# Expert 1's first eight slices in one visit of each token block instead of two, in a newly written order

## The chip, the cores and the metric

The kernel runs on one core of a Trainium2 chip. Its engines are named as the profile names them: PE (TensorE, matrix products), DVE (VectorE), ACT (ScalarE), POOL (GpSimd) and SP (SyncE, which issues all the transfers here). The time is the device time of one execution in microseconds (us); the median of several runs counts. Beside it stands the profile of one execution.

## What is computed

Causal attention with a bias from a running sum, then two feed-forward experts one after the other, on 2304 tokens of width 512:

```python
# q, k, v: [4, 8, 576, 64]; s: [4, 8, 576]
s_pos = np.maximum(s, 0.0)
cum = np.cumsum(s_pos, axis=-1)
bias = -(cum[:, :, :, None] - cum[:, :, None, :])
scores = np.where(causal, -1000000000.0, scores + np.minimum(bias, 0.0))
...
x = attention output as [2304, 512]
# expert 1: w_in [512, 2048], w_out [2048, 512]
h = x @ w_in
x = (h - np.tanh(h)) @ w_out
# expert 2: w_in [512, 1024], w_out [1024, 512]
h = x @ w_in
solu = h * softmax(h)
out = (layer_norm(solu) * g_ln) @ w_out
```

All products keep nearly full 32-bit precision: an operand is split into a high and a low part, and each product is three matmuls (high by high, high by low, low by high).

## The kernel before

**Attention.** There are 16 pairs of heads (four pairs for each of four batch items). They make 20 jobs: the first item's four pairs are done in two jobs each (jobs 0 to 3 take its first 256 tokens, 4 to 7 the rest), the other twelve pairs in one each (8 to 19). A job goes through its query rows 64 at a time: scores on PE (L715, masked by L723), the bias and the row minimum on DVE (L732), the exponential with its sum on ACT (L743), the reciprocal on DVE (L656, L659), the scaling on POOL (L747), transposes on PE (L781), copied out by ACT (tile pt, L294), and then weighed by v on PE (L821). The result goes out to memory (tensor xd).

**Expert 1.** The tokens are cut into nine blocks of 256, the inner width of 2048 into sixteen slices of 128. A block and a slice together are 24 matmuls: 12 for h (L868, "h part") and 12 that add into the output in the accumulator acc (L891, "x2 part"), with tanh on ACT (L873), the difference on DVE (L877), the high part by ACT (L294, tile gh) and the low part by DVE or POOL (L313, L314) between the two. The weights come as 64-bit numbers and are converted slice by slice, by ACT, DVE and now and then POOL (tiles cd, ct; wih, wil, woh, wol), early in the kernel for slices 0 to 7, later for 8 to 15.

While attention still runs there is room in memory for the weights of slices 0 to 7 alone. They are gone through in visits: `VISITS = ((0, 4), (4, 8))` means that every block is visited twice, once for slices 0 to 3 and once for 4 to 7. A visit loads the block of x from xd (tile xb, L860; block 0's first visit finds it in place), and at its end `keep_part` reads acc: the first visit copies it to the tile xp (`keep`, on ACT) and stores it to the tensor pd (L959); the second loads it back (L940), adds acc to it on DVE (L953) and stores it again. There is a single acc, so a visit's first x2 part waits until the one before it has been read out. After attention the slices 8 to 15 follow in a visit of their own (accumulator big), which loads the kept sum for the last time and goes straight on to expert 2 (L1016 and L1134 on PE).

**The order.** Nothing at run time decides the order. `schedule` makes all the steps with what they depend on, and the table `ORDER` of some 3300 numbers, written into the kernel, says in which order their instructions are issued, so what each engine does one after the other. A `+20` in it means 20 matmuls on a tile of zeros (L558), which keep PE busy where it is expected to wait. The costs in the code (`t_score`, `t_pe` and the like) belong to the planning of such a table; the order issued is that of the table alone.

Of the kernel before, what the change touches and what calls it, by code (L numbers as in the profile page):

```python
# [9 lines left out]
F32R = mybir.dt.float32r  # L10
# [30 lines left out]
VISITS = ((0, 4), (4, 8))  # L41
FA = 8
LT = ("cd", "cu")
TB = 256
# [5 lines left out]
0 f 3 u i l x 49 4i 7x p r +20 13 10 1u 2i 16 86 1a 1c 1x 39 bu 2l 4d 6 2p 1f 20 3c 4l 2r 23 1i 4f 1l 89 3f 2u 26 2x  # L50
29 bx 3i 81 +7 1o 3l 83 30 1r ff +1 2c 9 3o 2f +1 33 bl 36 +1 3r 3u +1 4r 31x 5i jc 4u 8f 3x 4y 50 5l 32l 8i 8m 5o 53
c 56 96 5r 8o 59 5u 66 8r 40 99 5x 9u 4o 43 9c al 8u 69 46 8x bp 6x 9x 6f a1 br c3 8c a3 5c 70 90 cu 5f a6 c6 c0 73 ca
di 6d a9 6i cx 60 ac 320 6l fc 76 ao e9 d0 6o 79 dl 63 7c af d3 cc 9f d6 9i 6r cf ar ec d9 7f ci f9 6u au 9l ax ef 323
+2 9o cl ei 7i el 93 b0 +2 7l 9r fi 32o 326 eo ai b3 7o 329 j9 co b6 er n9 7r dc cr b9 eu 32c r6 df dr 7u 32r fl bc du
32u 32f bf gc 32x hi 32i dx 330 bi e0 gf 333 fo 339 gi fs 336 jf fu hr fx j6 +7 ji +1 k9 hl g0 ho gl g3 v3 hu gr 11o
gp dp +4 g6 n6 gu hx e3 gx h0 i0 e6 i3 g9 +4 ex h9 if r3 33c h3 hc i6 h6 +1 ii 33f hf v0 33i i9 f0 35x il f3 33l +1 io
ic 3cl ir 33o 33r f6 ki iu 3co km 33u ko n3 jl 3cr jr 33x kc lf 3cu ju jp jx kf 3cx 50l k0 nf kr ix ku lo l6 k3 j0 189
3du li k6 kx lr ll j3 l0 lu 3d0 lx l3 m0 m3 11l o6 360 363 3d3 186 l9 mc 3d6 3d9 m6 366 lc mf 3dc m9 369 ml mi 36c mo
pc 36f nc ni o9 no mr 36i r0 oc pl 340 nr nm nu of nx 359 pf ol rc po 1er pi s3 oj oo 343 or mu 346 o0 pr p3 mx 1eu
349 o3 p6 ou pu px n0 p9 34c ox q0 34f ux v9 34i p0 q3 q9 3ec q6 11i sc sg si s6 rf 399 s9 t9 rj sl rl so ro sr 35c rr  # L60
11u 1lf qi tc ru ql qc ti 1lc tf t0 rx tl t3 qf 35f 35i su to qo 35l sx tr t6 35o s0 tu 34l 35r tx r9 vc w0 qr u6 12l
w3 vi w9 w6 u0 qu 35v wf vl u9 vo wi u3 vg uf vr wl qx 11x uc 121 wo 12u 13r ui 12o wx 130 v6 wd vu 12y 123 140 x0 vx
wr 12r 144 159 126 13u x3 129 133 13x 136 12c 16f wu 15i 13i 146 139 15m 15o 11r 149 12f 15c 13c 14c 13l 16o 12i 14o
13f 16i 13o x6 15f 14f 16r 14r 1s0 34o 15r xf 14i yo 15u 16u xj 34r 15x x9 183 xl 18f 34u ul 166 16l yr yx 1rx 14l xc
34x 1eo yu xo 350 14u 160 uo xr 18c 16x 169 z1 170 xu 353 ur 14x 356 163 uu 16c 173 196 150 xx 153 39c 3df y3 y0 39f
z3 17c z6 36l 18i 1f0 39i 3di yc z9 156 18m 18o 19f zc 199 19l 17l 18r 3dl 3dx zl 18u 19c 19j 17o 18x 19o yf 19r 39l
3do y6 3e0 19u yi 190 176 3dr 193 1ex 17f 1a3 y9 3e3 179 1f3 3ef 39o 17i 1l9 1f7 1f9 1fc 3e6 1ac 1ff 39r 3e9 379 1fi
1bu 3er 39u 36o 3h0 1al 17r 1ap 1ar 1af yl 1bx 1ai 1c3 1c0 1c7 1au 36r 1c9 1ax 19x 1li 36u zf 1b9 1cc 17u zo 1cf 1a0
17x zi 1fl 1b0 1a6 1bc 1fo 36x 1a9 1b3 1bf 1ll 180 1cr 1fr 1b6 1lo 1gx zr 370 1lu 1if 1ci 1g0 3b9 373 1h0 1lx 1bi 376
1g6 1h3 1m0 1io 1cl 1m3 37c 3ei 1ls 1is 1bl 37f 1iu 1bo 1h6 1br 1co 1ha 1m6 37i 1hc 1cu 1fu 1mc 37l 1m9 1cx 3eu 1hf  # L70
37o 1fx 3el 1hi 1ml 37x 1hu 1mf 1ii 37r 3f9 1hl 1g9 1mr 1gc 1mp 37u 1il 1gf 1ho 1ix 1mi 3fo 1g4 1go 1j0 1mu 3ex 3eo
# [167 lines left out]
def t_turn(n, k=1):  # L239
    return t_pe(109.0 * k, 128 * k)  # L240
# [1077 lines left out]
```

## Time and profile before

| | |
|---|---|
| median of 3 runs | 781.69 us (779.96 to 782.26) |
| the profiled execution, its own time | 778.94 us |
| its span, first to last instruction | 777.2 us |
| PE busy | 764.8 us of the span (98%) |
| PE weight loads busy | 676.8 us (87%) |
| DVE / ACT / POOL busy | 565.0 / 409.8 / 119.5 us |
| moved by DMA | 111.90 MB |
| granted PE clock | 1.00 throughout |

The busy time of an engine is the union of its instructions' records. The span lies within the profiled execution's own time; 1.74 us are around it. The profiled execution was somewhat faster than the median of the three timed ones, by 0.35%.

### The profile page before, as it was taken

What the parts mean: (1) busy time and instruction counts of PE and PEld (TensorE: products, weight loads), DVE (VectorE), ACT (ScalarE), POOL (GpSimd) and SP (SyncE); (2) the same over time, 40 slices, a digit from 0 to 9 for tenths busy, and PEclk for the clock granted to TensorE, in tenths of its full rate; (3) what the DMA queues carried; (4) which work ended last, traced back from release to release, by engine and by line L of the source; (5) the groups of instructions that cost most, each with busy time, mean ns of one, the idle gap of its engine ahead of it and who ended that gap; (6) DMA issues with size and microseconds to landing.
All of it is one profiled execution on the core that took longest, in us unless ns stands there. A gap on an engine that the chain in (4) does not pass through costs nothing.

```text
span 777.2 us, 16641 instructions
## 1 busy us (share of the span) xinstructions
PE 764.8 (98%) x6239; PEld 676.8 (87%) x6239; DVE 565.0 (73%) x1647; ACT 409.8 (53%) x1030; POOL 119.5 (15%) x193
## 2 busy tenths in 40 slices
PE   8899999999999999999999999999999999999997
PEld 5566788879889899999999898898888899989986
DVE  6888989654564458786699998869496755586783
ACT  6789989775665545454465663423243332343431
POOL 3235354431230200000000000001020001010000
PEclk9999999999999999999999999999999999999999
DMA  7999979874444278876535522112000310110001
GB/s 202 293 302 257 316 235 314 258 209 158 154 140 155 85 252 266 262 261 215 180 123 181 167 83 55 35 48 82 28 28 28 96 55 14 42 55 28 20 36 41
DMA packets 90033, 111.90 MB, mean 144 GB/s; under 512 B 11792, under 2 KB 74256, under 8 KB 89952
## 3 DMA queue, kind: packets, MB, share of 16 engines
q1 hardware_dynamic: 89952, 110.83, 46.2%
q8 instruction: 49, 0.80, 0.4%
q14 instruction: 32, 0.26, 0.1%
HBM read 87.11 MB, written 23.70 MB: 143 GB/s over the span
## 4 chain that ended last, share of the span: by engine, by line
PE 88%; DVE 5%; ACT 2%; DMA 2%; issue 1%; SPq 1%; POOL 0%; DVEq 0%; ACTq 0%; POOLq 0%
PE t L868 23%; PE big L891 13%; PE t L1134 12%; PE acc L891 11%; PE t L821 6%; PE big L1016 6%; PE t L781 5%; PE t L715 5%; PE b L1016 4%; PE t L1120 2%; ACT U L743 1%; DMA bc<-cum_d 1%; DMA cum_d<-pt 1%; ACT pt L294 1%; DVE U L732 1%
## 5 line engine op out<-in xcount | busy, mean ns | idle before, releaser
L868 PE MATMUL t<-xb,wih 128*128 128x256 f32 x1152 | 202.5, 279 | 0.0
L868 PEld LDWEIGHTS t<-xb,wih 128*128 128x128 f32 x1152 | 175.0, 188 | 1.7 <-DVE r L656 0.2
L868 PE MATMUL t<-xb,wil 128*128 128x256 f32 x576 | 159.5, 277 | 0.0
L868 PEld LDWEIGHTS t<-xb,wil 128*128 128x128 f32 x576 | 108.3, 188 | 0.0
L747 POOL TENSOR_SCALAR U<-U,r 128x64 f32<-128x64 f32 (+8 forms) x144 | 82.8, 589 | 163.5 <-DVE r L659 50.2
L891 PE MATMUL acc<-gh,woh 128*128 128x256 f32 x576 | 102.6, 280 | 0.8 <-DVE xp L953 0.7
L891 PE MATMUL big<-gh,woh 128*128 128x256 f32 x576 | 101.0, 278 | 0.0
L873 ACT ACTIVATE th<-t 128x256 f32<-128x256 f32 x144 | 54.7, 381 | 77.1 <-PE t L868 69.7
L877 DVE TENSOR_TENSOR g<-t,th 128x256 f32<-128x256 f32 x144 | 59.5, 417 | 46.6 <-ACT th L873 45.3
L294 ACT CAST gh<-g 128x256 fp32r<-128x256 f32 x144 | 58.1, 406 | 65.1 <-DVE g L877 32.4
L743 ACT ACTIVATE U<-U,m 128x64 f32<-128x64 f32 (+8 forms) x144 | 80.1, 558 | 21.2 <-DVE m L732 20.7
L891 PEld LDWEIGHTS big<-gh,woh 128*128 128x128 f32 x576 | 87.8, 188 | 1.0
L891 PEld LDWEIGHTS acc<-gh,woh 128*128 128x128 f32 x576 | 87.0, 188 | 1.7 <-ACT th L873 0.8
L891 PE MATMUL acc<-gh,wol 128*128 128x256 f32 x288 | 79.8, 277 | 0.4 <-DVE wol L313 0.4
L891 PE MATMUL big<-gh,wol 128*128 128x256 f32 x288 | 79.9, 277 | 0.0
L313 DVE TENSOR_TENSOR gh<-g,gh 128x256 fp32r<-128x256 f32 x124 | 54.0, 439 | 28.2 <-ACT gh L294 27.1
L732 DVE CUSTOM_DVE_ANT_0 U<-bc,t 128x64 f32<-128x64 f32 (+8 forms) x144 | 60.2, 441 | 8.3 <-PE t L723 6.6
L314 POOL TENSOR_TENSOR gh<-g,gh 128x256 fp32r<-128x256 f32 x20 | 16.5, 827 | 316.9 <-ACT gh L294 249.6
L294 ACT COPY pt<-t 128x512 f32<-128x512 f32 (+4 forms) x160 | 60.0, 428 | 7.2 <-PE t L781 6.4
L715 PE MATMUL t<-kn,q 64*64 64x288 f32 (+8 forms) x640 | 58.9, 422 | 2.3 <-DVE wol L313 1.3
L891 PEld LDWEIGHTS acc<-gh,wol 128*128 128x128 f32 x288 | 54.1, 188 | 0.6 <-DVE wol L313 0.6
L891 PEld LDWEIGHTS big<-gh,wol 128*128 128x128 f32 x288 | 54.2, 188 | 0.0
(114 smaller groups left out, 1433.8 us busy)
## 6 DMA issues: line engine op xcount, KB each, us to landing
xb<-xd SPq DMA_DIRECT2D x17, 1024.0 KB, 6.1
cd<-in_moe_w_in_dram SPq DMA_DIRECT2D x24, 512.0 KB, 4.8
cd<-in_moe_w_out_dram SPq DMA_DIRECT2D x24, 512.0 KB, 5.0
bc<-cum_d SPq DMA_DIRECT2D x32, 288.0 KB, 6.4
pd<-xp SPq DMA_DIRECT2D x18, 512.0 KB, 3.8
xp<-pd SPq DMA_DIRECT2D x18, 512.0 KB, 3.6
xd<-xs SPq DMA_DIRECT2D x16, 320.0 KB, 4.5
kn<-in_k_dram SPq DMA_DIRECT2D x16, 288.0 KB, 6.6
```

The source lines that it names most:

```text
L294: then(nc.scalar.copy(o, i) if scale == 1.0 else nc.scalar.activation(out=o, in_=i, func=AF.Copy, scale=scale))
L313: return self.any([("dve", t_dve(n, pair=True), lambda: nc.vector.tensor_tensor(*views(), op), "diff-dve"), ("pool", t_pool(n) + split, la ...
L715: nc.tensor.matmul(X[a][c, :z - a], lhsT=V["q"][r, o:o + 64], rhs=V["k"][r, a:z], start=True, stop=True, skip_group_check=True)
L732: nc.vector.tensor_tensor_reduce(out=X["u"][:, a:z], in0=V["bc"][:, n, a:z], in1=X[b][:, a - b:z - b], scale=-0.125, scalar=X["m"] if "m" ...
L743: nc.scalar.activation(out=X["u"][:, :nk], in_=X["u"][:, :nk], func=AF.Exp, scale=-1.0, bias=X["m"], accum_out=Y["s"][:, n:n + 1])
L747: eng.tensor_scalar(X["u"][:, :nk], X["u"][:, :nk], Y["r"][:, n:n + 1], 1.0, ALU.mult, ALU.mult)
L868: nc.tensor.matmul(ps, lhsT=w[l][:, k, f * 128:f * 128 + 128], rhs=xb[:, r, k, :], start=k == 0 and x == 0, stop=k == 3 and x == 2)
L873: nc.scalar.activation(out=X["th", f], in_=X["h", f], func=AF.Tanh)
L877: nc.vector.tensor_tensor(X["g", f], X["h", f], X["th", f], ALU.subtract)
L891: nc.tensor.matmul(X["acc"][:, m, :], lhsT=w[l][:, f, m * 128:m * 128 + 128], rhs=X["gh", f][:, r, :], start=f == c0 and m % 2 == 0 and x ...
L1016: i = nc.tensor.matmul(o, lhsT=self.x2[j][:, l, x, k], rhs=r[:, b, k, :], start=start and k == 0 and n == 0, stop=k == 1 and n == 2, skip_ ...
L1134: nc.tensor.matmul(X["po"], lhsT=X["lt", k // 4][:, l, k % 4, :], rhs=r[:, k, :], start=k == 0 and a == 0, stop=k == 7 and a == 2)
```

## The change

`VISITS` has one entry in place of two: each block goes through slices 0 to 7 in one visit. So there are nine visits and not eighteen before slices 8 to 15: nine loads of x fewer, and no kept sum is loaded back and added in this part, nor stored a second time; what is stored is the copy of acc after eight slices. Which of two pools a block of x lies in is counted from the other end. The costs used in planning are other numbers (they issue nothing), and the table ORDER is a new one, with 47 matmuls on zeros where there were 53. The products, the conversions of weights, attention and expert 2 have the same steps as before, in another order.

```diff
-VISITS = ((0, 4), (4, 8))
+VISITS = ((0, 8),)
...
-0 f 3 u i l x 49 4i 7x p r +20 13 10 1u 2i 16 86 1a 1c 1x 39 bu 2l 4d 6 2p 1f 20 3c 4l 2r 23 1i 4f 1l 89 3f 2u 26 2x
...
 def t_score(n, rows):
-    t = 1.6667 * n + 119.0 if rows == 1 else {192: 393.0, 320: 599.0, 448: 868.0, 576: 1090.0}[n]
+    t = 1.6667 * n + (160.0 if n < 128 else 180.0 if n < 256 else 150.0) if rows == 1 else {192: 535.0, 320: 685.0, 448: 912.0, 576: 1150.0}[n]
...
     def x_tile(self):
         n, self.nx = self.nx, self.nx + 1
-        return self.sb(self.xo if n % 2 and n < len(VISITS) * self.NB else self.mo, [128, 2, 4, TB], "xb", F32R, 1)
+        return self.sb(self.xo if n % 2 == 0 and n < len(VISITS) * self.NB else self.mo, [128, 2, 4, TB], "xb", F32R, 1)
...
-                s = add("pe", t_pe(1370.0, 12 * TB), lambda f=f: h_part(f), ld + [w["ready"][2 * f]] + list(deps), acq=("ps",),
+                s = add("pe", t_pe(1372.0, 12 * TB), lambda f=f: h_part(f), ld + [w["ready"][2 * f]] + list(deps), acq=("ps",),
```

The order shows what moves in three places. Line numbers are two smaller in the changed kernel. First the transfers that SP issues in the middle of attention, before: xd is where attention's results lie, xb a block of x, pd the kept sums.

```order
L834 DMA xd_73<-xs 256x1x256
L959 DMA pd_77<-xp 128x1024
L940 DMA xp<-pd_75 128x1024
L860 DMA xb<-xd_72 128x8x256
L588 DMA v<-in_v_dram 128x4x128
L590 DMA v<-in_v_dram 64x128
L834 DMA xd_73<-xs 256x1x320
L860 DMA xb<-xd_72 128x8x256
L834 DMA xd_74<-xs 256x1x256
L602 DMA bc<-cum_d 64x1152 x2
L959 DMA pd_75<-xp 128x1024
```

And about the same place, where the third block's sum is stored, now:

```order
L832 DMA xd_73<-xs 256x1x320
L832 DMA xd_73<-xs 256x1x256
L957 DMA pd_77<-xp 128x1024
L586 DMA v<-in_v_dram 128x4x128
L588 DMA v<-in_v_dram 64x128
L832 DMA xd_73<-xs 256x1x320
L832 DMA xd_74<-xs 256x1x256
L832 DMA xd_73<-xs 256x1x256
L600 DMA bc<-cum_d 64x1152 x2
```

The load of the kept sum, the second load of the same block and the second store of pd_75 are gone; the rest of the queue has closed up.

Second, ACT some way ahead of the weighing of job 10's second part. Before, the first accumulator had been copied out here and the second block had begun (th and gh are expert 1's, U and pt attention's, wih and ct the weights'):

```order
L743 ACTIVATE U,s<-U,m 128x128
L294 COPY xp<-acc 128x1024
L294 CAST wih_95<-ct 128x4x128
L743 ACTIVATE U,s<-U,m 128x192
L743 ACTIVATE U,s<-U,m 128x384
L743 ACTIVATE U,s<-U,m 128x128
L873 ACTIVATE th<-t 128x256
L294 COPY pt_1767<-t 128x4x64
L873 ACTIVATE th<-t 128x256
L294 CAST gh<-g 128x256
L873 ACTIVATE th<-t 128x256
L294 CAST gh<-g 128x256 x2
```

ACT now, at the same weight's conversion:

```order
L741 ACTIVATE U,s<-U,m 128x384
L741 ACTIVATE U,s<-U,m 128x448
L292 CAST wih_95<-ct 128x4x128
L292 COPY pt_1836<-t 128x4x64
L741 ACTIVATE U,s<-U,m 128x512
L415 ACTIVATE ct<-cd 128x512
L292 CAST xs<-t 128x256
L741 ACTIVATE U,s<-U,m 128x320
L292 COPY pt_1855<-t 128x2x64
L741 ACTIVATE U,s<-U,m 128x576
L741 ACTIVATE U,s<-U,m 128x256
L871 ACTIVATE th<-t 128x256
```

Attention has moved ahead of expert 1 here. Counted over the whole order up to that weighing on PE, expert 1 has had 9 h parts and 8 x2 parts before, 5 and 4 now; ACT has 198 steps ahead of it and not 207 (four tanh, five casts of gh, one copy of acc and one cast of a weight fewer, one exponential and one cast of xs more).

Third, DVE after attention, before: here the second visits' sums are added between the conversions of weights.

```order
L877 TENSOR_TENSOR g<-t,th 128x256
L399 TENSOR_SCALAR ct<-ct 128x512
L953 TENSOR_TENSOR xp<-acc,xp 128x1024
L402 TENSOR_SCALAR ct<-ct 128x512
L399 TENSOR_SCALAR ct<-ct 128x512
L405 SCALAR_TENSOR_TENSOR ct<-cd,ct 128x512
```

Now the accumulator is read by ACT, and DVE has no such row before slices 8 to 15. ACT there:

```order
L871 ACTIVATE th<-t 128x256
L292 CAST gh<-g 128x256
L292 COPY xp<-acc 128x1024
L871 ACTIVATE th<-t 128x256
L292 CAST woh_4949<-ct 128x512
```

The reading of acc has moved from DVE's queue, behind a conversion step, to ACT's, behind a cast of gh.

## Rows read from the trace of the kernel before

**Rows 1.** The page, part 1: busy us (share of the span) xinstructions.

```profile
PE 764.8 (98%) x6239; PEld 676.8 (87%) x6239; DVE 565.0 (73%) x1647; ACT 409.8 (53%) x1030; POOL 119.5 (15%) x193
```

**Rows 2.** Busy time by stretch: PE, PEld, DVE, ACT, POOL, PEclk, DMA share, GB/s.

```profile
34.50:113.80 79.30, 77.61 (x800) 59.24 (x800) 69.23 (x271) 69.25 (x203) 34.55 (x54) 1.00 0.96 280
0.00:60.00 60.00, 54.06 (x505) 36.84 (x506) 46.54 (x193) 44.24 (x131) 21.97 (x48) 1.00 0.94 265
60.00:140.00 80.00, 79.41 (x858) 61.98 (x857) 70.61 (x280) 71.99 (x217) 37.34 (x57) 1.00 0.96 282
140.00:280.00 140.00, 139.55 (x1393) 121.88 (x1392) 72.26 (x285) 85.82 (x256) 32.55 (x59) 1.00 0.52 158
280.00:360.00 80.00, 79.20 (x695) 78.67 (x694) 64.52 (x135) 41.30 (x92) 2.03 (x2) 1.00 0.83 271
360.00:480.00 120.00, 119.58 (x976) 116.06 (x975) 105.78 (x232) 65.22 (x139) 5.37 (x6) 1.00 0.45 143
480.00:777.20 297.20, 292.98 (x1824) 261.36 (x1823) 205.28 (x528) 101.21 (x198) 20.26 (x21) 1.00 0.13 42
```

**Rows 3.** The same view, the densest stretch for ACT.

```profile
60.00:100.00 40.00, 39.48 (x429) 29.17 (x428) 35.37 (x161) 38.23 (x124) 18.37 (x33) 1.00 1.02 295
```

**Rows 4.** PE's waits: engine, line, waited for: us in total, times, longest.

```profile
PE t L781 <- POOL U L747: 1.8, 5, 0.5
PE t L715 <- DVE wol L313: 1.3, 1, 1.3
...
PE acc L891 <- DVE xp L953: 0.7, 1, 0.7
PE t L715 <- DMA kn<-in_k_dram: 0.5, 1, 0.5
```

**Rows 5.** PE in order of time: start, us, form, count [idle before].

```profile
297.11 0.28 PE L891 MATMUL acc<-gh,wol 128*128 128x256 f32 x1
...
300.85 0.28 PE L891 MATMUL acc<-gh,wol 128*128 128x256 f32 x1
```

**Rows 6.** All instructions on the tile xp: ns least/median/most, first to last start.

```profile
L959 SPq DMA_DIRECT2D pd<-xp x18: 319/331/1453, 97.5 to 374.5; - x18
L940 SPq DMA_DIRECT2D xp<-pd x18: 320/327/486, 124.8 to 700.7; - x18
L294 ACT COPY xp<-acc x9: 987/1012/1020, 96.5 to 364.5; 128x1024 f32<-128x1024 f32 x9
L953 DVE TENSOR_TENSOR xp<-acc,xp x9: 1212/1218/1225, 143.2 to 373.2; 128x1024 f32<-128x1024 f32 x9
```

**Rows 7.** PE at the one long wait for the accumulator.

```profile
336.21 0.28 PE L868 MATMUL t<-xb,wil 128*128 128x256 f32 x1
337.15 0.47 PE L891 MATMUL acc<-gh,woh 128*128 128x256 f32 x2 [0.66 <-DVE xp L953]
```

**Rows 8.** DVE at that wait.

```profile
334.95 0.92 DVE L399 TENSOR_SCALAR ct<-ct 128x512 f32<-128x512 f32 x1
335.79 1.21 DVE L953 TENSOR_TENSOR xp<-acc,xp 128x1024 f32<-128x1024 f32 x1
```

**Rows 9.** PE at the start.

```profile
1.10 4.45 PE L558 MATMUL acc<-junk 128*128 128x256 bf16 x20 [1.10 <-POOL junk L553]
5.48 0.48 PE L715 MATMUL t<-kn,q 64*64 64x64 f32 x4
...
7.44 0.94 PE L558 MATMUL acc<-junk 128*128 128x256 bf16 x7
8.90 0.33 PE L781 MATMUL t<-idn,U 128*128 128x128 f32 x1 [0.52 <-POOL U L747]
```

**Rows 10.** Tiles th and gh from 34.5 us to the weighing at 113.8.

```profile
L873 ACT ACTIVATE th<-t x9: 371/383/400, 36.2 to 107.7; 128x256 f32<-128x256 f32 x9
L294 ACT CAST gh<-g x9: 387/407/424, 38.0 to 110.0; 128x256 fp32r<-128x256 f32 x9
```

**Rows 11.** PE where job 10's second part is weighed.

```profile
113.78 2.79 PE L821 MATMUL t<-pt,v 128*64 128x320 f32 x22
```

More of the change, by code (lines that the diff above doesn't have):

```diff
@@ L55 @@
[L55 to L59, printed above, removed]
@@ new lines @@
+1li 1gc 1bc 37f 1fo 1m6 373 1go 1hf 1cl 1hi 1cu 37i 1m9 3b9 1bf 1hu 1gr 1cx 1if 376 1gu 1gf 1co 1mc 37l 17u 1gi 1hl
+17x 3fc 1gl 1ml 180 1mf 1mr 1ii 1mi 1d0 1io 1il 37o 1iu 1mu 1ho 1mp 37x 1mx 1d3 37r 1n0 1ni 1yl 1n9 1hr 1ix 1d9 1d6
+1yi 1i3 37u 3bc 1nr 1nc 1i6 1j0 1n3 1nv 3ef 1dc 1nx 1jc 1nl 1ru 1n6 1j3 1df 1i9 3bf 1jl 1no 1di 1is 3bi 1ic 3ei 1dl
+3bl 380 256 1nf 1dx 1ju 1jo 253 1do 1e0 1jx 1jr 383 1yf 1dr 3el 1e3 1e6 386 1yr 1e9 3bo 1s6 1du 389 3br 39x 1ec 1o0
+38c 3eo 1k0 1o3 3bu 38l 38f 1of 1k3 1s9 1k6 1sf 1sd 1hx 1s3 1k9 1ef 1si 1sl 1j6 1i0 1ei 1ki 1jf 1j9 1el 1kc 3er 1ji
@@ new lines @@
+3h9 3ar 3gx 3cf 3h0 3au 3h3 3ho 3ci 3hc 213 3ax 216 3i6 3h6 3hr 3b0 3hf 3b3 3hu 3io 219 3i9 200 3b6 21l 203 10c 10f
+3j6 20f 3ir 21c 206 10i 3gf 10r 209 10l 3hi 20i 20c 3hl 10o 21o 3ic 3gi 21r 3j9 20l 3jo 3hx 3gl 3i0 3iu 3k6 3go 3jr
+3l3 3i3 3li 3if 3ii 3jc 3lx 3k9 3il 3j3 3ix 3j0 3ju 3jl 3l6 3jf 3ji 3kc 3k3 3jx 3ll 3k0 3l9 3kl 3m0 3kf 3ki 3lo 3ko
+3lc 3lf 3m3 3kr 3lr 3lu 10u 3m6 110 21f 3ku 3m9 3mf 3kx 21i 113 10x 3mc 3mi 3ml 116 3mo 3mr 226 2bu 119 11c 23c 229
+11f 22f 22c 1sx 2ox 22j 23l 21u 22l 23f 2ou 3mu 21x 22o 23o 23i 22r 1t6 2i6 22u 220 1tc 1t0 233 3nc 1t3 223 1ta 23r
@@ L161 @@
+796 7ec 79a 786 7ei 789 7el 79c 7eo 7eu 78c 79f 7er 79i 7ff 7ex 78f 7f0 7f3 78i 7f6 79u 7fo 7f9 79l 7fc 79x 79o 79r
+7fi 7a0 7fr 7a3 7fl 7a6 7a9 7g3 7fu 7g0 6px 7fx 6po 6y9 6pr 6q0 6pu 7g6 6q3 7g9 7gl 6yc 7go 7gc 7gr 6yf 7gu 6yi 7gx
+7h0 7gf 6yl 7h3 7h9 6yo 7h6 6q6 7gi 7hd 7if 7ho 7hf 6q9 7hi 7hr 7hl 6qc 7hu 7ii 7il 6qf 7io 7hx 6qi 7ir 6ql 7iu 7i0
+7ix 7j0 7j4 7jf 7j6 7i3 7j9 7ji 7jl 7i6 7jc 7jo 7i9 7ic 7jr 7ju 7jx 7k0 7k3
 """
@@ L792, in finish @@
                 start = i in (self.jobs[jb][1], 5) and c0 == 0
-                s = add("pe", t_turn(128, c1 - c0), turn, [t, X["pad"]] + ([] if start else [self.pt_first[g]]),
+                s = add("pe", t_pe({1: 104.0, 2: 226.0, 3: 300.0, 4: 436.0}[c1 - c0], 128 * (c1 - c0)), turn, [t, X["pad"]] + ([] if start else [self.pt_first[g]]),
                         acq=("ps", f"pt{g}") if start else ("ps",), rel=("U",) if c1 == nb else ())
@@ L1022, in pe @@
         def pe(go, deps, acq=(), rel=()):
-            s = add("pe", t_pe(1366.0, 3072), go, deps + list(self.w2_all), acq=acq, rel=rel)
+            s = add("pe", t_pe(1380.0, 3072), go, deps + list(self.w2_all), acq=acq, rel=rel)
             s.after = [self.h2_last] if self.h2_last else []
@@ L1157, in expert2 @@
         for n in range(2):
-            a = add("pe", t_turn(128, 4), lambda n=n: turn(n), [s], acq=("ps", LT[n]), rel=("ct",) if n else ())
+            a = add("pe", t_pe(395.0, 512), lambda n=n: turn(n), [s], acq=("ps", LT[n]), rel=("ct",) if n else ())
             a.mode = (1, 1)
```

206 lines of the change are left out of this document (98 added, 108 removed).

## The prediction

> **What bounds the kernel now.** Read the page's busy times first: PE is busy 764.8 of 777.2 us, the next engine, DVE, 565.0 [rows 1]. Busy stretches by time come next. From 60 us to the end of attention and on to 480 us PE is short of the whole stretch by little: 0.59 us of 80, 0.45 of 140, 0.80 of 80, 0.42 of 120; the last stretch lacks 4.2 us, which is the way of the last rows out of the kernel. Only the first 60 us lack much, 5.94 us, 1.10 of them before the first matmul [rows 2, 9]. So 12.4 us are open in the whole span, some 8 of them in places that another order could fill. The list of PE's waits names what they are: attention's chain (transposes that wait for POOL's scaling, 1.8 us in five waits), DVE held up by a weight conversion (1.3), the accumulator not yet read out (0.7), a load of k (0.5) [rows 4].
>
> Busy PE is also PE at its pace: from 297.11 to 300.85 us stand 33 matmuls of the x2 parts, so 113 ns each from start to start, in the middle of expert 1 [rows 5]. A part of 12 takes 1.36 us. Expert 1's first eight slices over nine blocks are 144 parts, 196 us, and the change removes none.
>
> **What the change removes.** Nine additions on DVE at 1.22 us (11.0 us), nine stores and nine loads of the kept sum, nine loads of x [rows 6]. DVE, with 565 us of 777, and the transfers do not bound the kernel, so what counts is where PE waited for them. That is one place: at 336.21 us an h part's last matmul starts, and the next x2 part starts at 337.15, with 0.66 us of idle put to the addition on DVE [rows 7]. The addition itself stood behind a conversion step of 0.92 us and ran from 335.79 to 337.00 [rows 8]. From start to start 0.94 us pass where 0.11 would do, so 0.83 us are lost. Now ACT reads acc with a copy of 1.01 us [rows 6], and ACT is busy 41.3 of 80 us there against DVE's 64.5 [rows 2]. I take -0.8; the bounds are 0, if ACT is as late as DVE was, and -0.8. All other accumulator handovers are hidden by h parts of the next visit already, and halving their number gives nothing. The nine loads of x and the eighteen transfers of sums cost SP some 0.33 to 0.6 us of issue each, and nothing on PE waits for SP there: 0.
>
> **What the new order changes in warm-ups.** Six matmuls on zeros fewer, five of them in the first run: 20 of them take 4.45 us, the scores begin at 5.48, without an idle gap [rows 9]. Five fewer would be 1.07 us if the scores' operands have landed by then. The order loads q and k ahead of the running sum's input, which was second; so the scores can start earlier, the row minimum behind them later. The next wait, 0.52 us for POOL, sits behind that chain [rows 9]. I take -0.5, half way; the bounds are 0 and -1.07.
>
> **What it changes in the first 60 us.** 5.94 us are idle there. The 1.10 ahead of the first matmul stay, 4.8 can be won. Up to the first parts of expert 1 the two orders run nearly alike (the same jobs, the same conversions), which speaks for little; a conversion row and a few transposes have other neighbours, which can remove or make a wait of 0.5 to 1.3 us such as those listed [rows 4]. Bounds 0 and -4.8; I take -1.5, nearer to the end that the likeness of the orders speaks for.
>
> **What it moves.** This is the term that can cost. Up to the weighing of job 10's second part, which starts at 113.78 us [rows 11], expert 1 had nine h and eight x2 parts on PE, now five and four. Eight parts of 1.36 us are 10.9 us that PE does later, so if PE set the pace alone it would come there in 79.3 - 10.9 = 68.4 us from 34.5 us on, and lose nothing, since the parts come back as one dense run later. But ACT has attention's exponentials and copies to do all the same. It is busy 69.25 us in this stretch [rows 2]; four tanh at 0.38 and five casts at 0.41 fall away [rows 10] and a copy at 1.01 [rows 6]; by the order's count one cast of a weight goes, and one exponential and one cast of xs come, which about cancel. That leaves 69.25 - 1.5 - 2.0 - 1.0 = 64.7 us of ACT in 68.4, a share of 95%. Has ACT been seen at that? From 60 to 100 us it is busy 38.23 of 40 us, 95.6%, with PE at 39.48 [rows 3]. At that share ACT needs 67.7 us: no loss. At its share over the whole stretch, 69.25 of 79.3 or 87.3%, it needs 74.1 us: 5.7 us lost. These are the bounds; the new stretch is all of the dense kind, nearest to the 60 to 100 us row, so I take 0. Above 89% the loss stays under 4.3 us.
>
> **Sum.** -0.8 - 0.5 - 1.5 + 0 = -2.8 us. The profiled execution took 778.94 us, so 776.1; the runs' median is 0.35% above it, 781.69, and in the median's measure this is 778.9 us. Calls of this kernel agree within some 0.3% (2.3 us), which is what a measurement can tell from no change; the forecast is just beyond it, at -0.36%.
>
> **Rivals.**
>
> *PE-bound, nothing to be had.* The idle of the first 60 us belongs to the first jobs' chain, which has the same steps; the warm-ups removed were standing in waits that stay. Then only the accumulator's 0.8 us is won, and a microsecond may be lost to ACT: 777 to 779 profiled, 780 to 782 in the median's measure. For it: PE's 98% and the likeness of the beginnings. Against it: 5.94 us lie open and the order there is new.
>
> *Slower: ACT sets the pace of attention up to about 110 us.* With eight parts of expert 1 taken out, PE has no work to put under ACT's chain, and waits for copies of transposes and for exponentials. The price is worked out above: up to 5.7 us, less the 2.8 of the forecast or less the 0.8 that is sure, so 779 to 784 profiled, 782 to 787 in the median's measure. It decides when ACT's share from 34.5 us to that weighing stays under some 88.5% (64.7 us in 73.1: 4.7 us lost, which leaves +1.9 to +3.9). For it: 87.3% is what that stretch has now, DVE is busy 69.2 of 79.3 beside it, and ACT's work comes in chains. Against it: 95.6% was reached over 40 us with the same kind of work.
>
> *More room than PE's busy time shows.* PE's weight loads are busy 59.24 of the 79.3 us up to that weighing, while from 280 to 360 us they are at 78.67 of 80 [rows 2]. If a third of those 20.1 us is hidden waiting that a better planned order removes, 6.7 us go on top: 769.4 profiled, 772.1 in the median's measure. For it: a matmul's record reaches over the next ones' starts, 0.28 us against a pace of 0.113 [rows 5], so short waits don't show as idle. Against it: attention's narrow matmuls (64-row tiles) load less per microsecond whatever the order, and the waits that are listed are short. The Trainium skill (Perfetto Trace Analysis, Identifying the Most-Contended Engine) says that matmul busy time is not a good measure of the room left on TensorE, since matmuls are pipelined, and wants the busy share of the weight loads in its place. By that rule 13% of this span would be open and not 1.6%; for expert 1 alone the trace disagrees, since both shares are full there.
>
> **How the numbers follow.** Forecast, 0.3% to 0.8% faster: 0.37. No change: 0.34. ACT's pace: 0.21, nearly all of it slower by over 0.3%. More room: 0.08. So faster 0.45, same 0.35, slower 0.20. The range goes from the forecast with the idle of the first 60 us taken at its bound (-0.8 - 1.07 - 4.8 = -6.7 us, 772.3 profiled, 775 in the median's measure) to ACT's rival near its upper end, 786; I take 774.5 to 786. The forecast's own range is 775 to 779.4.
>
> **What would show it.** In the profile after: DVE has no addition into xp from acc, and the accumulator's wait near 336 us is gone; if a wait of some 0.7 us for ACT's copy of acc stands there, that term is wrong. PE's idle in the first 60 us is about 4 us; if it is near 6, the third term is wrong. PE's first scores start at about 4.5 us, not 5.5. Job 10's second part is weighed at about 103 us (113.8 less 10.9); if it comes after 107, ACT's rival holds, and ACT's busy share up to there tells how far. PE's busy share from 140 to 480 us stays above 99%. The prediction would be wrong in sign if the dense run of expert 1 that now follows at about 105 to 140 us waited for weights: all sixteen halves of the eight slices' weights have to be converted by then, on DVE, for a single block, where before the second visit could wait.

## The result, and the profile after

The changed kernel takes 784.64 us (median of 5 runs, 784.24 to 789.41) against 782.26 us for the kernel before (779.96 to 783.09): a ratio of 1.0054, 95% interval 1.0028 to 1.008. It is slower: by 2.4 us between the medians, by 0.54% (some 4 us) by the ratio. Forecast was 2.8 us less. The profiled execution took 784.54 us, its span is 782.8 us.

The page's busy times, which answer to [rows 1]:

```profile
PE 767.9 (98%) x6233; PEld 677.3 (87%) x6233; DVE 551.8 (70%) x1637; ACT 409.3 (52%) x1029; POOL 119.9 (15%) x195
```

DVE has lost its 13 us, DMA moves 93.01 MB and not 111.90, and PE, with six products on zeros fewer, is busy 3.1 us longer and idle 2.5 us longer (782.8 - 767.9 = 14.9 against 12.4). The work taken away was taken from engines that had room.

Where PE is idle now, in the view of busy time by stretch, which answers to [rows 2] (columns as there):

```profile
0.00:60.00 60.00, 52.68 (x490) 35.26 (x494) 45.13 (x185) 43.34 (x128) 20.87 (x46) 0.97 0.96 257
60.00:120.00 60.00, 56.64 (x608) 39.29 (x601) 51.86 (x231) 54.48 (x172) 30.62 (x49) 1.00 0.93 269
120.00:280.00 160.00, 159.91 (x1595) 141.60 (x1594) 83.07 (x337) 100.16 (x294) 38.34 (x69) 1.00 0.39 116
280.00:360.00 80.00, 80.00 (x703) 77.26 (x701) 56.19 (x124) 41.41 (x93) 0.00 (x0) 1.00 0.57 177
31.97:109.34 77.37, 71.80 (x738) 50.08 (x736) 65.77 (x271) 68.00 (x202) 35.18 (x54) 1.00 0.96 269
```

From 120 to 480 us next to nothing is idle; from 280 to 360 us, where before lacked 0.80 us, PE is full. But from 60 to 120 us 3.36 us are open, where before from 60 all the way to 140 us lacked 0.59 [rows 2], and the first 60 us lack 7.32 in place of 5.94. The last row runs from expert 1's first h part to the weighing of job 10's second part, the stretch that the prediction priced; it begins 2.5 us earlier than in before [rows 2] and at an earlier place in attention's work, so more of attention lies in it. The waits up to 140 us answer to [rows 4]:

```profile
PE t L779 <- POOL U L745: 5.2, 9, 1.1
PE t L779 <- ACT pt L292: 1.2, 3, 0.6
...
PE t L713 <- DVE m L730: 0.6, 1, 0.6
PE t L819 <- ACT pt L292: 0.5, 1, 0.5
```

No wait for the accumulator is among them. They are attention's own chain: a transpose waits until POOL has scaled its rows, 5.2 us in nine waits where [rows 4] has 1.8 in five. What such a wait looks like, PE in order of time:

```profile
103.27 0.50 PE L866 MATMUL t<-xb,wih 128*128 128x256 f32 x2
...
104.67 0.28 PE L866 MATMUL t<-xb,wil 128*128 128x256 f32 x1
104.89 1.20 PE L713 MATMUL t<-kn,q 64*64 64x512 f32 x12
105.79 0.32 PE L721 MATMUL t<-mask,unit 64*64 64x64 bf16 x4
106.95 0.66 PE L779 MATMUL t<-idx,U 128*128 128x128 f32 x4 [0.84 <-POOL U L745]
...
109.34 1.03 PE L819 MATMUL t<-pt,v 128*64 128x320 f32 x6 [0.49 <-ACT pt L292]
...
126.16 0.48 PE L866 MATMUL t<-xb,wih 128*128 128x256 f32 x2
```

One h part (block 0's slice 4) ends at 104.9, scores and masks follow, and then PE has nothing it could do but wait. The row at 109.34 is the weighing of job 10's second part, which waits too. The next part of expert 1 comes at 118.7 us. In before parts of expert 1 stand between such steps here.

Why they do not stand here now is seen on DVE in order of time, where the low half of a slice's weights is the last step of their conversion:

```profile
102.13 0.68 DVE L311 TENSOR_TENSOR wil<-ct,wih 128x512 fp32r<-128x512 f32 x1
...
125.25 1.45 DVE L311 TENSOR_TENSOR wil<-ct,wih 128x512 fp32r<-128x512 f32 x2
```

Slice 4's weights for h are ready at 102.8 us, and its h part starts at 103.27. Slice 5's (the first of the two in the second row) are ready about 125.9 us, and the h part that needs them, the last row on PE above, starts at 126.16. So block 0's slices 4 and 5 stand as early as their weights allow. Slice 7's weights for h are ready before slice 5's, at 111.3 us, but its h part keeps its place behind slice 6's, at 129.07. And with one visit per block no other block may come before them: the program puts the h parts in the sequence of the visits, and the single acc does the same for the x2 parts. In before, block 1's slices 0 to 3, whose weights had been there since 92.7 us, were at hand just then.

The view of one line's instructions by stretch counts this. From 94 to 118 us (span, PE's busy time and products, weight loads), for the h part and the x2 part each; in the kernel before, profiled a second time:

```profile
94.00:118.00 24.00, 7.85 (x60) 7.29 (x60) 1.00 0.81 251
94.00:118.00 24.00, 7.95 (x64) 7.31 (x63) 1.00 0.81 251
```

and in the changed kernel:

```profile
94.00:118.00 24.00, 1.68 (x12) 1.48 (x12) 1.00 0.89 263
94.00:118.00 24.00, 1.66 (x12) 1.54 (x12) 1.00 0.89 263
```

124 products of expert 1, ten parts, against 24, two parts.

### The profile page after: what moved, and what is told of

Read it like the earlier page. It is cut to its first block, busy times and chain, and to the rows that moved or that the text cites. A ratio compares the mean times of both kernels' runs of the same rounds, so it can differ in the third digit from the quotient of the medians.

```text
span 782.8 us, 16547 instructions
## 1 busy us (share of the span) xinstructions
PE 767.9 (98%) x6233; PEld 677.3 (87%) x6233; DVE 551.8 (70%) x1637; ACT 409.3 (52%) x1029; POOL 119.9 (15%) x195
## 2 busy tenths in 40 slices
DMA packets 74960, 93.01 MB, mean 119 GB/s; under 512 B 9264, under 2 KB 61488, under 8 KB 74880
## 4 chain that ended last, share of the span: by engine, by line
PE 90%; DVE 3%; ACT 3%; issue 1%; POOL 1%; DMA 1%; SPq 1%; POOLq 0%; DVEq 0%; ACTq 0%
PE t L866 25%; PE acc L889 13%; PE t L1132 12%; PE big L889 12%; PE big L1014 6%; PE t L819 6%; PE t L779 5%; PE b L1014 4%; PE t L713 4%; PE t L1118 2%; ACT U L741 1%; POOL U L745 1%; ACT pt L292 1%; DVE U L730 1%; PE t L721 0%
## 5 line engine op out<-in xcount | busy, mean ns | idle before, releaser
L745 POOL TENSOR_SCALAR U<-U,r 128x384 f32<-128x384 f32 (+8 forms) x144 | 84.2, 598 | 185.4 <-DVE r L657 95.9
L741 ACT ACTIVATE U<-U,m 128x256 f32<-128x256 f32 (+8 forms) x144 | 80.0, 558 | 19.6 <-DVE m L730 19.2
L311 DVE TENSOR_TENSOR gh<-g,gh 128x256 fp32r<-128x256 f32 x133 | 57.7, 435 | 45.7 <-ACT gh L292 45.4
L730 DVE CUSTOM_DVE_ANT_0 U<-bc,t 128x256 f32<-128x256 f32 (+8 forms) x144 | 59.8, 443 | 6.1 <-PE t L721 4.3
L819 PE MATMUL t<-pt,v 128*64 128x320 f32 (+4 forms) x448 | 52.9, 370 | 0.9 <-ACT pt L292 0.5
```

The source lines that it names most:

```text
L311: return self.any([("dve", t_dve(n, pair=True), lambda: nc.vector.tensor_tensor(*views(), op), "diff-dve"), ("pool", t_pool(n) + split, la ...
L730: nc.vector.tensor_tensor_reduce(out=X["u"][:, a:z], in0=V["bc"][:, n, a:z], in1=X[b][:, a - b:z - b], scale=-0.125, scalar=X["m"] if "m" ...
L741: nc.scalar.activation(out=X["u"][:, :nk], in_=X["u"][:, :nk], func=AF.Exp, scale=-1.0, bias=X["m"], accum_out=Y["s"][:, n:n + 1])
L745: eng.tensor_scalar(X["u"][:, :nk], X["u"][:, :nk], Y["r"][:, n:n + 1], 1.0, ALU.mult, ALU.mult)
L819: nc.tensor.matmul(X["x"][r, q0:gw], lhsT=V["v"][:kc, c, r], rhs=V["pt", g][:kc, cc, h, r0:r0 + gw - q0], start=c == 0, stop=c == len(part ...
```

## Experiments

Two theories. **Cover:** one visit per block takes away the parts of block 1 that PE had under attention while slices 4 to 7 were still being converted; then attention's chain, which is long and not dense, leaves PE waiting. **Order or length:** the removal itself costs (a longer visit, ACT's copy), or the new order of the start and of attention does. All ratios are to the kernel before, run on the same chip. Expert 1's parts from 94 to 118 us, PE's idle time from 80 to 120 us (40 us less its busy time there) and in the whole span (span less the page's busy time), and the result:

| kernel | products 94-118 us | idle 80-120 us | idle, whole span | ratio (95% interval) |
|---|---|---|---|---|
| before (second profile) | 124 | 0.00 | 11.6 | 1 |
| blocks 3 to 8 merged | 123 | 0.00 | 11.1 | 0.9955 (0.9931 to 0.998) |
| all but block 0 merged | 123 | 0.00 | 12.0 | 0.9974 (0.9947 to 1.0) |
| nothing merged, visits in a row | 32 | 7.28 | 21.6 | 1.021 (1.018 to 1.024) |
| all merged, order of before | 24 | 7.71 | 26.0 | 1.0216 (1.0181 to 1.0252) |
| nothing merged, half of the cover | 75 | 4.62 | 21.9 | 1.0214 (1.017 to 1.0257) |
| the changed kernel | 24 | 1.35 | 14.9 | 1.0054 (1.0028 to 1.008) |

The last row has an order made for its lack of parts: part of its waiting stands ahead of 80 us (2.00 us from 60 to 80 us, before 0.52). In all the others attention's steps and the weights' conversions are issued in the sequence of before on every engine; only expert 1's parts and what belongs to their visits move.

**The removal alone.** Two kernels keep the order of before. The first merges only visits that lay one behind the other; the second merges block 1's and block 2's as well, for which block 2's second visit and block 0's change places. RUNS lists visits as (which of VISITS, block).

```diff
-VISITS = ((0, 4), (4, 8))
+VISITS = ((0, 4), (4, 8), (0, 8))
+RUNS = ((0, 0), (0, 1), (1, 1), (0, 2), (1, 0), (1, 2), (2, 3), (2, 4), (2, 5), (2, 6), (2, 7), (2, 8))
...
-        for at, v, j in sorted(visits):
+        for v, j in RUNS:
```

> The order of before, number by number, with blocks 3 to 8 in one visit of eight slices (in that order their two visits already follow one another) and blocks 0 to 2 in two, as before. What falls out is six reads of x, six second loads and additions of the kept sum; the copy of acc by ACT takes the addition's place. Theory 'the loss comes from the new order, the removal itself gives about what was forecast': the wait near 336 us is gone and nothing else moves, so the span is 777.2 - 0.8 to 777.2 - 1.3, some 776.2 us, ratio 0.9985. Rival 'the longer visit itself costs' (ACT's copy is later than the addition was, or the longer visit holds its block of x too long): the span stays at 777.2 or grows by up to 1 us, ratio 1.000 to 1.001.

Measured: 0.9955, span 774.5 us. PE issues the same 6239 products in the same order as before, so the two traces can be compared product by product: number 3080, at 317.6 us in before, starts 0.52 us earlier, number 3300, at 343.9 us, 1.86 us earlier. So the wait for the accumulator of [rows 7], with two wider distances between products at 341.7 us, cost 1.34 us in that profile, not 0.8. Nothing took its place here; ACT's copy of acc costs PE nothing at the same handover:

```profile
335.69 0.28 PE L868 MATMUL t<-xb,wil 128*128 128x256 f32 x1
335.80 0.39 PE L891 MATMUL acc<-gh,woh 128*128 128x256 f32 x2
```

But this is not a gain of every execution. In the second profile of before, where nothing is merged either, no such wait stands: PE is busy 120.00 of 120 us from 300 to 420 us (the row is in the last section), and the same 220 products take 25.91 us, 118 ns each. The 0.52 us ahead of number 3080 are left of 0.7 us from the first 60 us, where the two orders are the same.

The ratio is better than 1.34 us alone (0.2%) would give, and its interval reaches to 0.998. Part of the reason lies in the single times. They fall into two groups in both kernels: before 7 of 34 at 777.90 to 779.73 us and the others from 781.35 us on, here 7 of 11 at 776.30 to 778.45 and 4 from 780.58 on. Between the lower groups' medians lie 1.6 us, between the upper ones' 1.1, so like with like 0.1% to 0.2%. The rest is that more executions fell into the lower group; whether merging has to do with that was not found.

```diff
+RUNS = ((0, 0), (2, 1), (2, 2), (1, 0), (2, 3), (2, 4), (2, 5), (2, 6), (2, 7), (2, 8))
```

> The order of before with only block 0 in two visits; blocks 1 to 8 in one. Block 1's two visits follow one another in the order of before anyway; block 2's second visit takes the place of block 0's second and the other way round. So all of the cover that block 1 gave while the weights of slices 4 to 7 were still being converted stays. Theory of the order: as with six blocks, some 776 us of span, ratio 0.998 to 0.999. Theory 'one visit per block cannot have the cover': this one keeps the cover, so it gives the same 776 and does not tell against it. Rival 'the longer visit itself costs': 777 to 778.5, ratio 1.000 to 1.002.

Measured: 0.9974, span 775.9 us, not slower. The longer visit costs nothing that can be measured in eight of nine blocks, and the rival (777 us or more) is out for these.

**The new order's beginning.** All blocks merged, the order of before up to a point, from there that of after (- the changed kernel's order, + these two kernels').

```diff
-f 0 3 x i u l 10 4i 49 7x p 86 r +15 13 1u 2i 39 bu 1x
+0 f 3 u i l x 49 4i 7x p r +20 13 10 1u 2i 16 86 1a 1c
...
```

> All blocks in one visit. The order is that of before up to the first h part of expert 1 (about 34 us; all 53 warm-up products stand there, 20 ahead of the first scores, and the loads in SP's old order), from there that of after. Theory 'the start's order costs 0.9 to 1.2 us, by the lower granted clock at 12 to 15 us and by the row minimum that starts later': the span is 782.8 - 1.2 = 781.6 us, the granted clock of the first 20 us is 1.00 again, and the ratio to before is 1.0035 to 1.004. Rival 'the loss is all in attention's order behind it, and a better start is eaten by the next wait': 782.8 us, ratio 1.005.

> All blocks in one visit. The order of before up to the place where block 1's first h part stood (some 82 us of PE's work, about 88 us on the clock), from there that of after, less what has been issued. Theory 'the loss is made of the start (1.2), attention's order from 41 to 81 us (2.9) and the missing cover behind 100 us (2.4)': the first two go, the third stays, span 782.8 - 4.1 = 778.7 us, ratio 1.001 to 1.002, with attention's waits for POOL and ACT at 100 to 120 us as in after. Rival 'PE's work that was moved back has to be paid wherever it is taken from, and attention's chain then sets the pace': what is won up to 88 us is lost again up to 120 us, span 781.5 to 783, ratio 1.005.

Measured: 1.0076 (1.0049 to 1.0102) and 1.0077 (1.0053 to 1.01), both no better than the changed kernel, so my own division of the loss (start 1.2, attention 2.9, cover 2.4) fell. The rivals were nearer; the spans, 784.4 and 787.4 us, are longer than even they said, the second in part because its products stand 118 ns apart from 300 to 420 us, of which the last section tells. Busy time from 60 to 80 and from 80 to 120 us of the second kernel:

```profile
60.00:80.00 20.00, 19.62 (x212) 12.61 (x214) 16.79 (x79) 19.04 (x61) 10.01 (x17) 1.00 1.00 260
80.00:120.00 40.00, 36.19 (x384) 25.95 (x385) 34.49 (x148) 35.14 (x110) 16.94 (x29) 1.00 0.90 266
```

With before's order up to 88 us PE is as dense there as in before (0.38 us idle against 2.00 in the changed kernel from 60 to 80 us), and from 80 to 120 us it pays 3.81 us. By putting attention elsewhere the idle time was moved here, not removed.

**The cover without the change.** Nothing is merged: all eighteen visits, kept sums and additions are there. Only block 0's second visit now follows its first, as in the changed kernel, so block 1 comes later.

```diff
+RUNS = ((0, 0), (1, 0), (0, 1), (1, 1), (0, 2), (1, 2), (0, 3), (1, 3), (0, 4), (1, 4), (0, 5), (1, 5), (0, 6),
+        (1, 6), (0, 7), (1, 7), (0, 8), (1, 8))
```

> Nothing is merged here: every block has its two visits, with kept sums, second reads and additions, and attention, the weights' conversions and expert 2 stand as in the order of before. Only the sequence of the visits is another: block 0's second visit follows its first (then block 1's two, block 2's two), so its parts fill the places in which before has block 1's first visit; those whose weights are not converted by then are moved back behind the conversion. From 94 to 126 us PE so gets two to three parts of expert 1 instead of ten. Theory 'cover: between 80 and 120 us attention leaves PE idle unless there are parts whose weights are there already, and these were block 1's slices 0 to 3': PE's idle time from 60 to 120 us, 0.52 us in before, grows to 3 to 4.5 us, the span to 780 to 782 us, ratio 1.004 to 1.006, though nothing of the change is in it. Rival 'it is the longer visit, or the new order of attention': 0.5 us of idle, 777 us, ratio 1.000.

Measured: 1.021, far more than either theory gave, in the direction of the cover; PE's idle time from 60 to 120 us is 7.80 us. PE at the place:

```profile
95.59 0.32 PE L724 MATMUL t<-mask,unit 64*64 64x64 bf16 x4
97.72 0.44 PE L782 MATMUL t<-idn,U 128*128 128x128 f32 x2 [1.81 <-POOL U L748]
98.09 1.75 PE L716 MATMUL t<-kn,q 64*64 64x512 f32 x12
99.37 0.51 PE L724 MATMUL t<-mask,unit 64*64 64x64 bf16 x4
99.82 0.47 PE L782 MATMUL t<-idn,U 128*128 128x128 f32 x1
104.28 1.11 PE L782 MATMUL t<-idx,U 128*128 128x128 f32 x4 [3.99 <-POOL U L748]
105.05 0.78 PE L869 MATMUL t<-xb,wih 128*128 128x256 f32 x2
105.62 0.41 PE L869 MATMUL t<-xb,wil 128*128 128x256 f32 x1
105.83 0.63 PE L869 MATMUL t<-xb,wih 128*128 128x256 f32 x2
106.26 0.41 PE L869 MATMUL t<-xb,wil 128*128 128x256 f32 x1
```

and in the second profile of before, the same attention steps:

```profile
95.74 0.32 PE L723 MATMUL t<-mask,unit 64*64 64x64 bf16 x4
95.99 0.50 PE L868 MATMUL t<-xb,wih 128*128 128x256 f32 x2
...
98.80 0.28 PE L868 MATMUL t<-xb,wil 128*128 128x256 f32 x1
98.92 0.38 PE L781 MATMUL t<-idn,U 128*128 128x128 f32 x2
```

Two h parts stand where 1.81 us of waiting are now. And no engine is at its limit in these 8.4 us (PE, PEld, DVE, ACT, POOL of 8.38 us):

```profile
95.90:104.28 8.38, 2.58 (x20) 1.25 (x20) 6.34 (x27) 6.66 (x19) 5.11 (x10) 0.66 0.71 263
```

So it is the length of the chain (scores, row minimum, exponential, reciprocal, scaling, transpose) that PE waits for, not the throughput of one engine.

All nine blocks merged, in the same sequence:

```diff
+RUNS = ((2, 0), (2, 1), (2, 2), (2, 3), (2, 4), (2, 5), (2, 6), (2, 7), (2, 8))
```

> The same order as in the kernel with two visits in a row, but with all nine blocks in one visit of eight slices: no kept sums, no second reads. Cover theory: idle of 3 to 4.5 us from 60 to 120 us, less the 1.3 us of the accumulator's wait near 336 us that the merged visits take away, so a span of 779 to 781 us, ratio 1.002 to 1.004. Rival 'the new order is at fault and not the one visit': the order is that of before but for the parts of blocks 0 to 2, so 776 us, ratio 0.998.

Measured: 1.0216, again far more than the cover theory gave, beside 1.021 for the unmerged one; merging changed nothing that can be measured, losing the cover changed 2%. With before and the kernel that merges all but block 0 these are the four combinations, as nearly as they can be had: a merge of all nine blocks has no cover. And since that merge costs 2.2% in the order of before and 0.5% in the new one, the new order is not where the loss comes from; it wins back most of it.

```diff
+VISITS = ((0, 4), (4, 8), (0, 8), (0, 2), (2, 8))
+RUNS = ((0, 0), (3, 1), (1, 0), (4, 1), (0, 2), (1, 2), (0, 3), (1, 3), (0, 4), (1, 4), (0, 5), (1, 5), (0, 6),
+        (1, 6), (0, 7), (1, 7), (0, 8), (1, 8))
```

> As in the kernel with two visits in a row (nothing merged, attention and conversions in the order of before), but block 1's first visit is cut to slices 0 and 1 and stands where before has it; its second has slices 2 to 7. So from 94 to 107 us PE gets six parts of expert 1 (two h and two x2 parts of block 1, one or two of block 0's slice 4); before has nine there, the kernel with two visits in a row two. Cover theory: the loss grows as the parts go, so this one lies between: the waits for POOL's scaled rows near 96 to 104 us are 1 to 3 us in place of 5.8, the granted clock from 100 to 120 us stays above 0.95, ratio 1.004 to 1.012. Rival 'it is the sequence of block 0's two visits, however many parts lie under attention': 1.018 to 1.024 as there.

Measured: 1.0214, no better: the rival's figure, not the theory's. At the place itself the parts count as the theory says: idle from 80 to 120 us is 4.62 us, between 0.00 and 7.28, and the clock holds.

```profile
100.00:120.00 20.00, 17.11 (x163) 13.24 (x162) 14.81 (x57) 15.03 (x42) 8.51 (x14) 1.00 0.75 234
```

But what was saved there was lost from 108 to 139 us in waits of 1.0 to 1.4 us for POOL and DVE, since there too expert 1's parts had been put off. Over the whole span PE idles 21.9 us, as much as with the visits in a row (21.6), and the ratio is the same. So the waiting that the parts put back covered at one place came up at another, and that the loss grows with the number of parts missing at the first is not shown.

**What the clock adds.** In the unmerged kernel without cover the granted clock falls behind the waits:

```profile
100.00:120.00 20.00, 14.53 (x116) 11.01 (x116) 14.30 (x46) 12.40 (x33) 8.40 (x12) 0.78 0.80 233
```

0.78 is a mean over the levels of 1.2 and 2.4 GHz; the h part behind the wait, at the lower one, has 0.21 us from product to product (105.62, 105.83, then two in 0.43). Here 8 and 18 products on zeros stand in the two waits, as `+8` and `+18` in ORDER; they write a bank of their own:

```diff
+            V["n"] += 1
+            if V["n"] in (54, 62):
+                V["late"] = self.bank([128, TB])
+            o = V["acc"][:, 0, :] if V["n"] < 54 else V["late"]
-            nc.tensor.matmul(V["acc"][:, 0, :], lhsT=self.junk[:, 0:128], rhs=self.junk, start=True, stop=True)
+            nc.tensor.matmul(o, lhsT=self.junk[:, 0:128], rhs=self.junk, start=True, stop=True)
```

> The kernel with two visits in a row, with 8 and 18 warm-up products put into the two waits of 1.81 and 3.99 us that opened at 95.9 and 100.3 us (they write a bank of their own). No work of the program moves. Its granted clock from 100 to 120 us was 0.78, and the twelve products of the next h part went at 0.21 us from start to start in place of 0.113. If the clock is what makes 5.8 us of waiting cost some 16 us, the clock is 1.00 there again, the waits themselves stay (now filled with products that count for nothing), and 0.22 of 20 us come back, 4.4 us: span 792 to 793 us, ratio 1.014 to 1.017. If the loss is the waits and what is late behind them: 797 us, 1.021.

Measured: 1.0207 (1.0167 to 1.0247), and the clock is 1.00 from 100 to 120 us; the span is 794.7 us in place of 796.9. Product by product PE gains 2.0 us at the two waits and in the h part behind them, half of what was expected, and loses 1.0 of them again in the next wait at 119 us; by the ratios the clock cannot be told from nothing. PE's idle time is the larger part of the loss: 21.6 us without these products against 11.6 in the second profile of before, 10.0 of the 15.5 us between the two spans. The rest is busy time at a lower pace; beyond the clock's share it was not divided.

**The changed kernel's start.** Five and two more products on zeros in its first waits.

```diff
-81 3i ff 3l +13 1o 30 4d 83 bl 2c 1r 3o 9 33 2f 36 +1 3r
+81 3i ff 3l +18 1o 30 4d 83 bl 2c 1r 3o 9 33 2f 36 +3 3r
```

> The changed kernel with seven more warm-up products, five of them in the 1.09 us that PE waits at 7.6 us and two in the 0.39 us at 10 us; nothing else is moved. There the granted clock of the first 20 us was 0.91, in before, with more warm-up products, 1.00. If that clock is paid for, 0.09 of 20 us, 1.8 us, come back: span 781 us, ratio 1.002 to 1.004. If the half pace at 12 to 15 us lay beside waits that stay (in the kernel with the start of before, clock 1.00, the span did not fall): 782 to 784 us, ratio 1.004 to 1.008.

Measured: 1.0103 (1.0071 to 1.0135), worse than both expectations and no better than the changed kernel. The clock of the first 20 us rose to 0.99, that of the next 20 fell to 0.92, so the loss was not won back by a faster clock at the very start. (The changed kernel itself, profiled again below, has 1.00 there and is no faster.)

**Two attempts to give cover back, both failed.** The changed kernel's order with block 0 split and block 1's slices 0 to 3 put between; and its order with the conversions in natural sequence and block 0's parts moved up to them:

```diff
+RUNS = ((0, 0), (2, 1), (1, 0), (2, 2), (2, 3), (2, 4), (2, 5), (2, 6), (2, 7), (2, 8))
```

```
conversions, 2f is w_in and 2f + 1 w_out of slice f
changed kernel: 0 1 2 6 3 5 4 11 7 8 14 9 10 12 15 13
here:           0 1 2 3 4 5 6 7 8 9 10 11 12 13 14 15
```

> The changed kernel's own order, with block 0 alone in two visits again: block 1's slices 0 to 3 (eight parts) are put between 81 and 107 us of PE's work, block 1's slices 4 to 7 take the places of block 0's, and block 0's last four slices follow behind. Cover theory: the idle from 100 to 120 us (1.34 us in the changed kernel) goes to under 0.3, the waits that do not show as idle there go too, and the span falls by 2 to 4 us, from 782.8 to about 780, ratio 0.999 to 1.002; what was lost before 80 us stays. Rival 'attention's order is at fault': idle as in the changed kernel, 782 us, ratio 1.005.

> All blocks in one visit, the changed kernel's order, but the sixteen conversions of weights in the sequence in which one block needs them (slice 0's two halves, slice 1's, and so on), and block 0's parts of slices 1 to 5 moved to where their weights are ready: some 47, 56, 64, 71, 80, 85, 92, 99, 102 us of PE's work. So ten to twelve parts lie under attention up to 105 us, not ten up to 98 and then none. Cover theory: idle from 100 to 120 us goes under 0.7 us, but one block has only two parts for each conversion, so some waits stay: span 780 to 782 us, ratio 1.001 to 1.004. Rival 'conversions do not gate, attention's chain is slow whatever lies under it': 783 us or more, ratio 1.005 or more.

Measured: 1.0211 (1.0181 to 1.0242) and 1.0388 (1.0356 to 1.0419). The first missed at the place itself: its idle time from 100 to 120 us is 1.56 us, where the theory gave under 0.3, because the parts put in wait themselves (0.74 us for DVE at 105.6 us) and so does a weighing. Later it waits 5.09 us at 147.9 us for a conversion that stood behind attention's steps on DVE and ACT. This may be my order's own fault; so the cover was not given back in the changed kernel's order, and this run does not support the theory. The second idles 2.41 us from 100 to 120 us in place of under 0.7 and waits for attention's chain in many places (POOL 6.94 us at 148.3 us). Neither shows that conversions in another sequence could save the single visit for block 0; that stays open.

**The two kernels, unchanged, profiled again,** once each.

> The kernel before, unchanged, profiled once more. In its first profile the products of the dense stretch from 300 to 420 us stand 113 ns apart; in some of the other kernels' profiles the same stretch, with the same work, stands at 118 ns for 100 us and more, at a granted clock of 1.00. Theory 'the pace is a matter of the execution and not of the order': this profile may show 118 ns in a stretch where the first showed 113, and then a span up to 6 us longer (4.4% of at most 140 us), some 783 us, with the same waits. Theory 'the pace belongs to the order': 113 ns in the same places, 777 to 778 us. Either way the first 60 us tell how much the start varies (the kernel with blocks 3 to 8 merged had the same order there and came 0.8 us earlier).

> The changed kernel, unchanged, profiled once more. Theory of the missing cover: PE's idle from 60 to 120 us is 3 to 4.5 us again (3.36 in the first profile), nearly all of it for POOL's scaled rows and ACT's copies. If that idle is an accident of one execution, it is under 1.5 us here. The granted clock of the first 20 us is 0.91 again if it belongs to the order, 1.00 if not.

Measured: spans 781.4 and 785.7 us, 4.3 us apart. The changed kernel's idle from 60 to 120 us is 3.40 us again, its clock in the first 20 us 1.00 and not 0.91, while its products from 32 to 111 us come about 0.3 us earlier than in the first profile: the idle belongs to the order, the clock does not. And the kernel before differs by 4.2 us from itself, of which the last section tells.

## Why the prediction was wrong

The step that failed is the one that it called the term that can cost: "nearest to the 60 to 100 us row, so I take 0". It asked whether ACT had throughput enough for attention without expert 1's parts, took it that ACT had, and so put the weighing of job 10's second part at about 103 us, the 10.9 us of eight parts earlier than before. It comes at 109.34: 6.5 us were lost up to there in place of 0, more even than the bound of 5.7. PE idles 10.7 us up to the weighing, 4.2 us more than in before, most of it in waits for attention's chain; the other 2.3 are busy time at a lower pace. (The 77.37 us from 31.97 to 109.34 are not to be set against the forecast of 68.4: 3.3 us more of ACT's work lie in them, 68.00 us and not 64.7, since expert 1 begins earlier.)

The weighing comes behind the 107 us from which the prediction said that its rival "ACT sets the pace" would hold, and ACT's share is 68.00 of 77.37, 87.9%, under the 88.5% that it named. So that rival gave the place and the time (782 to 787, measured 784.64), but the time in part by luck, since its price rests on the wrong cause: where the cover is wholly gone ACT is busy 6.66 of 8.38 us, and PE still waits. The 95.6% of [rows 3] were reached with expert 1's parts between attention's steps. They were read as what ACT can do alone; the runs show them only for the two kinds of work together.

The Trainium skill (Perfetto Trace Analysis, Optimization Strategy) says that a kernel whose most-contended engine changes over time may gain by interleaving its regimes. The runs here agree, from the other side: with block 1's parts interleaved the ratios are 1 (before) and 0.9974, without them 1.021 and 1.0216.

The other terms. **Accumulator, -0.8:** too small for the profile it was read from, 1.34 us, but no sure gain: the second profile of before has no such wait to win. **Warm-ups, -0.5, and the first 60 us, -1.5:** wrong. The scores start at 4.41 us as forecast, but the transposes behind them wait 1.09 us for POOL, and idle in the first 60 us is 7.32 (6.91 in the second profile) against 5.94: 1.38 us more, with 1.3 us less of warm-ups (six at 0.22), so nothing won:

```profile
4.41 0.48 PE L713 MATMUL t<-kn,q 64*64 64x64 f32 x4
...
8.68 1.08 PE L779 MATMUL t<-idn,U 128*128 128x128 f32 x3 [1.09 <-POOL U L745]
```

That the two orders "run nearly alike" there was the better half of that step. **PE above 99% from 140 to 480 us:** right, 339.82 of 340. **Weights:** the sign was to be wrong if the dense run waited for weights. It does not wait; the weights act earlier, by deciding which parts may stand under attention at all. The prediction looked for a wait, and the price lay in the place.

The sum: span +5.6 us in the first pair of profiles, +4.3 in the second, 0.54% or 4.2 us in the runs. The first pair is the better comparison, since both its profiles have the shorter distance of the last section from 300 to 420 us; in the second pair each has the longer one for another length of time. Idle accounts for 2.5 and 3.3 us of these (14.9 in both changed profiles against 12.4 and 11.6). The rest is busy time at a lower pace, 4.4 and 2.3 us if the warm-ups are taken out; how much of that is short waits inside attention was not divided. Whether another new order could do without the loss was not tried beyond the two failed attempts. That it is the missing cover is shown in the order of before, by the four combinations; for the changed kernel's own 0.5% it is read from its waits and from when its weights are ready.

What beats both kernels is a part of the change: merging only where the two visits already followed one another, 0.45% faster than before (0.2 to 0.7%), of which like with like 0.1% to 0.2% are left.

## What to carry to other kernels

Before work is moved out of a stretch in which a long chain runs, count what it covers: an engine at 95% there says what the mixture does, and need not say what the chain does alone. When visits or loops are merged, ask for each what it needs to have ready and what else could run until then; merge where this is nothing, and keep the split where the first pieces fill the wait for the next ones' weights. One profile of each kernel is not enough for differences of half a per cent, nor to take a single wait of 0.7 us for a sure gain.

## What the hardware did that was not expected

The same products of the dense stretch go at two distances, 113 and 118 ns, at a granted clock of 1.00 in both cases, and one execution stays at one of them for 100 us and more. From 300 to 420 us, PE without any idle time, all of it expert 1: first the second profile of before, then the changed kernel.

```profile
300.00:420.00 120.00, 120.00 (x1021) 120.00 (x1020) 95.38 (x206) 61.40 (x135) 2.50 (x3) 1.00 0.65 215
```

```profile
300.00:420.00 120.00, 120.00 (x1056) 119.73 (x1055) 99.27 (x219) 65.63 (x145) 2.17 (x1) 1.00 0.52 165
```

120 us for 1021 products are 117.5 ns each, for 1056 113.6. It is not the order's doing: the first profile of before has 113 ns there [rows 5], with each product's record at 276 ns where the second has 281:

```profile
L868 PE MATMUL t<-xb,wih x323: 281/281/281, 302.2 to 419.9; 128*128 128x256 f32 x162
```

Up to product 1540, at 159 us, the two profiles of before lie within 0.3 us of each other; at product 4180, at 449 us, they are 4.21 us apart, and stay so to the end. The changed kernel's second profile has the wide distance from 340 us on and is 2.97 us longer than its first. What sets the distance was not found. The difference is as large as the spread of the runs (779.96 to 783.09 us before) and as the step between their two groups; the two profiled executions of before, 778.94 us with the shorter distance and 783.15 us with the longer, fall one into each. So it is likely what parts them, and why a profile may lie 3 us off the median, but for the other executions the distance was not read.
